# Six parts of each query and key row laid out in DRAM by the stores, and a group's rows loaded in two transfers

## The chip, the cores and the metric

The kernel runs on one core of a Trainium2 chip. The core has a matrix engine (TensorE, PE in the profile), a vector engine (VectorE, DVE), an activation engine (ScalarE, ACT), a general engine (GpSimd, POOL) and SyncE (SP), from whose queue nearly all DMA transfers of this kernel are issued, one after the other; the transfers themselves are carried by 16 DMA engines. The metric is the device time of one execution in microseconds, and the median of several executions is compared.

## The reference

Two independent layers are computed and their results set side by side along the last axis. A is attention in four segments with a compressive memory, for 32 heads of 18 dimensions over 2048 positions; B is a Fourier mixing layer over the same shape (2048 x 576).

```python
def _A_ref(x, wq, wk, wv, wo, beta):
    B, S, D = x.shape
    H = 32; Dh = D // H; N = 4; L = S // N
    # q, k, v: x @ w, as (B, H, N, L, Dh)
    ...
    for s in range(N):
        qs, ks, vs = q[:, :, s], k[:, :, s], v[:, :, s]
        logits = jnp.einsum("bhqd,bhkd->bhqk", qs, ks) * scale + mask
        p = _softmax(logits, axis=-1)
        a_dot = jnp.einsum("bhqk,bhkd->bhqd", p, vs)
        pq = phi(qs)
        num = jnp.einsum("bhld,bhde->bhle", pq, M)
        den = jnp.einsum("bhld,bhd->bhl", pq, z)[..., None] + 1e-6
        o = g * (num / den) + (1.0 - g) * a_dot
        outs.append(o)
        pk = phi(ks)
        M = M + jnp.einsum("bhld,bhle->bhde", pk, vs)
        z = z + jnp.einsum("bhld->bhd", pk)
    ...
    return o @ wo

def _B_ref(x, dft_seq_re, dft_seq_im, dft_hid_re, dft_hid_im):
    a = jnp.einsum("bsd,ed->bse", x, dft_hid_re)
    b = jnp.einsum("bsd,ed->bse", x, dft_hid_im)
    return jnp.einsum("ts,bse->bte", dft_seq_re, a) - jnp.einsum("ts,bse->bte", dft_seq_im, b)
```

All inputs and the output are float32, so the kernel splits operands into high and low parts and adds several products.

## The kernel before

**Projections** (lines 435 to 479). For each of the four segments s of 512 positions, nine tiles m of query and key rows are projected (`project_qk`, line 236: m from 0 to 3 queries, 4 to 7 keys, 8 the last 64 rows of both) and then the values of four blocks j of 128 positions (`project_v`, line 276), from the second segment on with the look-ups in the memory (`lookup`, line 331) between them. The result of a tile m stands in a PSUM bank (four banks with the tag "acc"), and ACT and POOL cut it into three bfloat16 parts that add up to it: `p[:, 0]` (line 247), `p[:, 1]` (256 or 258) and `p[:, 2]` (259). `p` has four buffers. The three parts go to DRAM in one store per tile, to `qd[s]` or `kd[s]`, of shape [576, 3, 512] (lines 261 to 264); the tile m = 8 has one store for each.

**Attention** (`attention`, line 805) works in 32 groups G of four heads, 8 groups for each segment, and 64 pairs of heads (two pairs to a group) plus four steps that drain the pipeline. Scores are one bfloat16 matmul over 108 rows for each piece of a head: the six products of parts that matter (query parts 0, 0, 1, 0, 2, 1 against key parts 0, 1, 0, 2, 0, 1; QPARTS and KPARTS, lines 32 and 33) are stacked below each other, 6 x 18 = 108 rows. `stack_load` (line 420) fetches this stack for a group: six transfers of 18 rows x 4 heads x 512 for the query stack `qs` and six for the key stack `ks`, each row 1 KB. There are four buffers of each; three more rows of `qs` take the maxima of the scores, which go through DRAM (`maxima_transpose`, line 719: a store `md<-mt` and later a load `qs<-md`), against rows of ones in `ks` that POOL sets (line 403).

A head with an even number is scored a second time with keys on the partitions (`t_fill`, line 727), for which it needs the maxima in `qs`; one with an odd number is scored again with queries on the partitions (`f_fill`), and its probabilities are transposed by a DMA transpose on SyncE (`f_turn`, line 706), which waits for both halves of `f_split_lo`, on POOL and on DVE. `pv` (line 765) multiplies the probabilities with the values `vst`, which the `values` part of `stack_load` fetches.

**Order.** The order on every engine is the order in which the program emits instructions. `later(n, fn)` (line 82) puts work n ticks off; `tick()` runs what is due. In the projections there is one tick for each tile m and each block j. In attention each step p has eight slots with a tick after each (lines 815 to 859), and after each slot a stretch of the Fourier layer (`dense`, line 573) is emitted until the shares of both agree; its inputs come through `c_load` (`craw`, four buffers, line 373) and are cut by `c_cut`. SyncE runs its queue strictly in order: a transfer that waits for an engine holds up all transfers emitted behind it.

`stack_load` is called for group 0 in the last segment after the seventh of the nine tiles (n = 6), with one query and one key part in each of the six following ticks (`each=1`), and in attention at the first slot of every even step p, for group p/2 + 1, with two of each in each of three ticks. The values of a group follow `lag` ticks after the call. `f_turn` is called in the last slot of a step.

Of the kernel before, what the change touches and what calls it, by code (L numbers as in the profile page):

```python
# [15 lines left out]
BF16 = mybir.dt.bfloat16  # L16
# [7 lines left out]
P = 128  # L24
# [4 lines left out]
HEAD0 = [0, 7, 14, 21, 24]  # L29
NPAIR = 108  # L30
BF16_ONES = float(np.array([0x3F803F80], np.uint32).view(np.float32)[0])
QPARTS = [0, 0, 1, 0, 2, 1]
KPARTS = [0, 1, 0, 2, 0, 1]


@with_exitstack
def infini_attention_and_fnet(ctx: ExitStack, tc: tile.TileContext, xT, wqk, w8, wv, wo, beta, xtT, cT, hT, out):
# [5 lines left out]
    dram = ctx.enter_context(tc.tile_pool(name="dram", bufs=1, space=DRAM))  # L43
    wide = ctx.enter_context(tc.tile_pool(name="wide", bufs=32))

    qd = [dram.tile([D, 3, L], BF16, name=f"qd{s}") for s in range(NSEG)]
    kd = [dram.tile([D, 3, L], BF16, name=f"kd{s}") for s in range(NSEG)]
    vd = [dram.tile([P, 4, 8, 220], BF16, name=f"vd{s}") for s in range(NSEG)]
    amd = [dram.tile([P, D], F32, name=f"amd{t}") for t in range(NT)]
    md = [dram.tile([24, P], BF16, name=f"md{g}") for g in range(32)]  # L50
# [171 lines left out]
    def open_qk(s):  # L222
# [4 lines left out]
        for a, b in zip(edges, edges[1:]):  # L227
# [5 lines left out]
            if s and a == 0:  # L233
                accumulate(3, (0, 1))

    def project_qk(s, m):
        if m in FIRST:
            o = FIRST.pop(m)
        else:
            o = ps.tile([P, L], F32, name="qk", tag="acc", bufs=4)  # L240
            chain(o, qk_terms(s, m))
        if m >= 4 and s < 3:
            KF[m] = sk.tile([P, L], F32, name="kf", bufs=5)
            act.activation(KF[m], o, AF.Copy)
        p = sb.tile([P, 3, L], BF16, name="p", bufs=4)
        r = sb.tile([P, L], F32, name="r", bufs=2)
        act.activation(p[:, 0], o, AF.Copy)
        dve.tensor_tensor(r, o, p[:, 0], OP.subtract)
        if s and (m < 4 or m == 8):
            n = P if m < 4 else 64  # L250
            c = m if m < 4 else 4
            phi(sb, "q", o[:n], n, pq_hi[:n, c], pq_lo[:n, c])

        def rest():
            if m in (5, 6, 7):
                pool.tensor_copy(p[:, 1], r)
            else:
                act.activation(p[:, 1], r, AF.Copy)
            pool.tensor_tensor(p[:, 2], r, p[:, 1], OP.subtract)
            if m < 8:  # L260
                later(1, dma, (qd if m < 4 else kd)[s][(m % 4) * P:(m % 4 + 1) * P], p)
            else:
                later(1, dma, qd[s][4 * P:], p[:64])
                later(1, dma, kd[s][4 * P:], p[64:])

        later(1, rest)

# [149 lines left out]

    NG = 32

    def stack_load(G, lag=39, each=2):  # L420
        if G >= NG:
            return
        s, g8 = divmod(G, 8)
        rows = slice(g8 * 72, g8 * 72 + 72)
        for buf, src, parts in ((qs_bufs[G % 4], qd[s], QPARTS), (ks_bufs[G % 4], kd[s], KPARTS)):
            for c, part in enumerate(parts):
                later(1 + c // each, dma, buf[18 * c:18 * c + 18],
                      src[rows, part, :].rearrange("(h d) t -> d h t", d=DH))

        def values():  # L430
            VS[G] = sa.tile([P, 4, 220], BF16, name="vst", bufs=2)
            dma(VS[G], vd[s][:, :, g8])
        later(lag, values)

    for s in range(NSEG):
        more = s < 3
        if s == 0:
            warm_up()
        open_qk(s)
        if s:  # L440
            memory()
        else:
            tick()
        for n, m in enumerate((0, 1, 2, 3, 8, 4, 5, 6, 7) if s else range(9)):
            project_qk(s, m)
            tick()
            if not more and n >= 5:
                h_split(0, n - 5)
            if s in (1, 2) and n >= 4:
                load_x(s + 1, n - 4)  # L450
            if not more and n == 0:
                for k in range(5):
                    h_load(0, k)
            if not more and n == 4:
                p1k.close()
                sr = ctx.enter_context(tc.tile_pool(name="sb2r", bufs=1, side="right", reuse_waits="tile"))
                attention_tiles()
            if not more and n in (5, 6):
                stacks(sr, n - 5)
            if not more and n == 5:  # L460
                c_load(0)
            if not more and n == 6:
                stack_load(0, 99, 1)
        for j in range(4):
            project_v(s, j, lookup(s, j) if s else iter(()))
            if more:
                k_natural(j)
            tick()
            for k in ((0, 1), (2, 3), (4,), ())[j] if s == 0 else ():
                load_x(1, k)  # L470
            if more and j in (1, 2):
                split_x(s + 1, j - 1)
            if not more and j < 3:
                h_split(0, 4) if j == 0 else c_cut(j - 1, dve)
            if not more:
                c_load(1 + j)
            if more and j:
                accumulate(j - 1)
# [326 lines left out]
    def attention():  # L805
        for p in range(NP + V_LAG):
            def even(lag, fn, *a):
                if 0 <= p - lag < NP:
                    fn(2 * (p - lag), *a)

            def odd(lag, fn, *a):
                if 0 <= p - lag < NP:
                    fn(2 * (p - lag) + 1, *a)

            if p == 2:
                stacks(sa, 2)
                stacks(sa, 3)
            if p == NP + 1:
                o_load(0)
                o_load(1)  # L820
            if p % 2 == 0:
                stack_load(p // 2 + 1)
            if p % 2 == 0 and 0 < p <= NP:
                maxima_transpose(p // 2 - 1)
            even(T_LAG + 1, t_lo, 0)
            even(0, s_fill, 0)
            odd(F_LAG + 1, f_exp, 2)
            odd(F_LAG + 1, f_split_hi)
            yield SLOTS[0]
            even(T_LAG, t_fill, 0)  # L830
            even(T_LAG, t_fill, 1)
            yield SLOTS[1]
            even(0, s_fill, 1)
            odd(F_LAG + 1, f_split_lo, pool, 512, 1280)
            yield SLOTS[2]
            even(V_LAG, pv)
            even(0, s_fill, 2)
            odd(F_LAG + 1, f_split_lo, dve, 0, 512)
            even(T_LAG, t_mask)
            yield SLOTS[3]  # L840
            odd(F_LAG, f_fill, 1)
            even(T_LAG, t_fill, 2)
            if p % 2 and p < NP:
                maxima(p // 2)
            yield SLOTS[4]
            odd(F_LAG, f_fill, 0)
            even(T_LAG, t_hi)
            yield SLOTS[5]
            odd(V_LAG, pv)
            odd(F_LAG, f_fill, 2)  # L850
            odd(F_LAG, f_exp, 1)
            even(T_LAG, t_lo, 1)
            even(T_LAG, t_lo, 2)
            yield SLOTS[6]
            odd(F_LAG, f_exp, 0)
            if p >= V_LAG:
                pv_out(p - V_LAG)
            odd(F_LAG + 1, f_turn)
            yield SLOTS[7]

    d = dense()
# [75 lines left out]
```

## Time and profile before

| | |
|---|---|
| median of three runs | 1028.67 us (1027.47 to 1031.02) |
| the profiled execution, its time | 1030.27 us |
| the profiled execution, span from first to last instruction | 1028.5 us |
| granted TensorE clock, mean over the span | 0.997 |
| TensorE busy | 1007.7 us (98%) |
| DVE, ACT, POOL busy | 705.9, 715.0, 624.2 us |
| stores of query and key parts (qd<-p, kd<-p) | 20 + 20 |
| loads of query and key stacks (qs<-qd, ks<-kd) | 192 + 192, of 72 KB |
| loads of maxima (qs<-md), DMA transposes (ptt<-hl) | 32, 64 |

In the rows of the timeline the first number is the start in us from the first instruction, the second the length, then engine, line, operation, output and inputs, the number of instructions merged into the row, and in brackets how long the engine had been idle and what released it. SPq is SyncE's queue; its rows are the times in which it issues a transfer, not those in which data move. In a table of windows the columns are the stretch, the busy time (with the number of instructions) of PE, PEld (weight loads), DVE, ACT and POOL, the granted clock of TensorE (PEclk), the mean busy share of the 16 DMA engines, and what they moved in GB/s. In a list of waits stand the total in us, the number of times and the longest.

### The profile page before, as it was taken

How to read it: one execution, taken by the hardware profiler on the slowest of the kernel's cores; microseconds unless marked ns; L12 is line 12 of the kernel's file. 1: busy time of each engine (PE TensorE's matmuls, PEld its weight loads, DVE VectorE, ACT ScalarE, POOL GpSimd, SP SyncE). 2: the span in 40 equal slices, each digit the busy share in tenths (PEclk: the TensorE clock that was granted, in tenths of full speed). 3: DMA queues.
4: the chain of work that ended last, by engine and by line, in shares of the span. 5: the costliest groups of instructions: out<-in, count | busy, mean ns of one | idle time of the engine just before them, and what ended most of it. 6: DMA issues, size and time to landing. Idle time of an engine off the chain costs nothing.

```text
span 1028.5 us, 25886 instructions
## 1 busy us (share of the span) xinstructions
PE 1007.7 (98%) x9464; PEld 942.5 (92%) x9464; DVE 705.9 (69%) x1903; ACT 715.0 (70%) x1654; POOL 624.2 (61%) x668
## 2 busy tenths in 40 slices
PE   9999999989999999999999999999999999999998
PEld 7989989889999999998998999999999889999998
DVE  6645557563677777778888777777777778885442
ACT  6657575653777787877878788877677777876333
POOL 2657575775666677676766867666667567666000
PEclk9999999998999999999999999999999999999999
DMA  7516243375568887898998987689998899977574
GB/s 250 186 65 204 88 159 147 128 242 151 154 157 190 199 207 197 210 218 193 221 215 194 217 188 182 164 202 226 224 217 195 202 242 234 235 176 182 156 209 137
DMA packets 287743, 194.46 MB, mean 189 GB/s; under 512 B 210496, under 2 KB 242816, under 8 KB 287616
## 3 DMA queue, kind: packets, MB, share of 16 engines
q1 hardware_dynamic: 287616, 192.81, 73.5%
q8 instruction: 74, 1.21, 0.5%
q14 instruction: 53, 0.43, 0.1%
HBM read 106.84 MB, written 43.97 MB: 147 GB/s over the span
## 4 chain that ended last, share of the span: by engine, by line
PE 83%; DMA 7%; ACT 2%; POOL 2%; DVE 2%; SPq 2%; issue 1%; POOLq 0%; ACTq 0%; DVEq 0%
PE d L493 31%; PE qk L78 6%; PE s L664 6%; PE d L78 6%; PE qk L230 5%; PE v L78 4%; PE pv L780 4%; PE d L539 3%; PE d L540 3%; PE d L541 3%; DMA qs<-md 2%; PE pv L781 2%; PE m L314 2%; DMA ptt<-hl 2%; DMA ks<-kd 2%; PE look L339 1%
## 5 line engine op out<-in xcount | busy, mean ns | idle before, releaser
L670 DVE CUSTOM_DVE_ANT_0 s<-s,causal 128x128 f32<-128x128 f32 (+3 forms) x512 | 251.7, 498 | 119.9 <-PE s L664 108.6
L393 POOL TENSOR_TENSOR clo<-craw,chi 128x512 fp32r<-128x512 f32 x158 | 209.6, 1327 | 161.4 <-ACT chi L388 128.1
L493 PE MATMUL d<-wide,chi 128*128 128x288 f32 x1408 | 266.7, 306 | 0.0
L493 PEld LDWEIGHTS d<-wide,chi 128*128 128x128 f32 x1408 | 212.3, 189 | 1.3 <-issue 0.2
L493 PE MATMUL d<-wide,clo 128*128 128x288 f32 x704 | 178.0, 319 | 0.0
L664 PE MATMUL s<-ks,qs 108*128 108x128 bf16 (+3 forms) x512 | 134.2, 304 | 6.7 <-DMA ks<-kd 4.3
L704 POOL TENSOR_TENSOR hl<-pf,hl 128x768 f16<-128x768 f32 x64 | 110.2, 1723 | 48.5 <-ACT hl L700 39.8
L693 ACT ACTIVATE pf<-s,nb 128x128 f32<-128x128 f32 (+3 forms) x256 | 128.3, 527 | 6.2
L493 PE MATMUL d<-ab,chi 128*128 128x288 f32 x640 | 126.1, 306 | 0.0
L748 ACT ACTIVATE phi<-t 128x384 f16<-128x384 f32 x128 | 62.3, 487 | 83.7 <-PE t L745 83.7
L493 PEld LDWEIGHTS d<-wide,clo 128*128 128x128 f32 x704 | 119.0, 189 | 1.0
L388 ACT ACTIVATE chi<-craw 128x512 fp32r<-128x512 f32 x160 | 100.6, 630 | 8.1 <-DMA craw<-cT 3.3
L763 DVE TENSOR_TENSOR plo<-pf,phi 128x384 f16<-128x384 f32 (+1 forms) x128 | 105.0, 821 | 0.0
L749 ACT ACTIVATE pf<-t 128x384 f32<-128x384 f32 (+1 forms) x192 | 100.1, 521 | 3.8 <-PE t L738 3.7
L493 PEld LDWEIGHTS d<-ab,chi 128*128 128x128 f32 x640 | 98.5, 189 | 0.4
L700 ACT ACTIVATE hl<-pf 128x768 f16<-128x768 f32 (+1 forms) x128 | 87.4, 729 | 2.0
L539 PE MATMUL d<-wide,chi 128*128 128x288 f32 x256 | 85.6, 334 | 0.0
L493 PE MATMUL d<-ab,clo 128*128 128x288 f32 x320 | 84.9, 314 | 0.0
L540 PE MATMUL d<-wide,chi 128*128 128x288 f32 x256 | 76.5, 299 | 0.0
L541 PE MATMUL d<-wide,clo 128*128 128x288 f32 x256 | 76.4, 299 | 0.0
L763 POOL TENSOR_TENSOR plo<-pf,phi 128x384 f16<-128x384 f32 x64 | 61.3, 957 | 11.5 <-ACT pf L749 10.7
L704 DVE TENSOR_TENSOR hl<-pf,hl 128x512 f16<-128x512 f32 x64 | 62.9, 982 | 0.7 <-ACT hl L700 0.5
(196 smaller groups left out, 2522.8 us busy)
## 6 DMA issues: line engine op xcount, KB each, us to landing
craw<-cT SPq DMA_DIRECT2D x128, 256.0 KB
qs<-qd SPq DMA_DIRECT2D x192, 72.0 KB
ks<-kd SPq DMA_DIRECT2D x192, 72.0 KB
craw<-xtT SPq DMA_DIRECT2D x32, 320.0 KB
out<-y SPq DMA_DIRECT2D x31, 288.0 KB
vd<-vs SPq DMA_DIRECT2D x16, 440.0 KB
vst<-vd SPq DMA_DIRECT2D x32, 220.0 KB
qd<-p SPq DMA_DIRECT2D x16, 384.0 KB
```

The costliest lines, as they stand in the source:

```text
L78: pe.matmul(o, a, b, start=n == 0, stop=n == len(terms) - 1)
L388: act.activation(hi, raw[:, :4], AF.Copy)
L393: engine.tensor_tensor(lo, raw[:, :4], hi.bitcast(F32), OP.subtract)
L493: pe.matmul(o[h], a, b[:, h * 288:h * 288 + 288], start=start, stop=stop)
L539: pe.matmul(o, xh[:, k], wl[k][:, cs], start=k == 0, stop=False)
L540: pe.matmul(o, xh[:, k], wh[k][:, cs], start=False, stop=False)
L541: pe.matmul(o, xl[:, k], wh[k][:, cs], start=False, stop=False)
L664: pe.matmul(o[:, c:c + w], q[:, i * P:w], k[:, :w], start=True, stop=True)
L670: dve.tensor_tensor_reduce(o[:, c:c + w], o[:, c:c + w], CAUSAL[0][:, L - w:], scale=scale, scalar=-LOWEST, op0=OP.add, op1=OP.min, accum_ ...
L693: act.activation(f[:, FIRST_COL[i]:FIRST_COL[i] + w], o[:, c:c + w], AF.Exp, bias=nb[:, i:i + 1], scale=-1.0)
L704: engine.tensor_tensor(hl[:, 1, a:b], f[:, a:b], hl[:, 0, a:b], OP.subtract)
L763: (pool if kind == 2 else dve).tensor_tensor(lo[:, a:b], f[:, a:b], hi[:, a:b], OP.subtract)
```

## The change

The arrays in DRAM get six parts for each row in place of three, in the order in which the stacks need them; the stores write a part as often as it occurs, with a source that repeats. The query stack's order is now 0, 1, 2, 0, 1, 0 and the key stack's 0, 0, 0, 1, 1, 2, which makes the same six products. In QPARTS and KPARTS each tuple is (first place, first part, number of parts, copies). In the first segment a query tile is stored once, with three parts, and each key part once; four transfers from DRAM to DRAM, emitted in the second segment after its first four tiles, fill the other places.

A group's stack is then 108 rows of DRAM at one step, and `stack_load` is one transfer for queries and one a tick later for keys. Its calls move: group 0 to the fifth tile of the last segment, group 1 to the first slot of step 0, the others from the first slot of an even step to the seventh slot of the odd step before it. `f_turn` moves from the end of the last slot to the start of the seventh, ahead of that call. `lag` becomes 41, two ticks more, as the call comes two ticks earlier. The stack buffers 2 and 3 are made at steps 1 and 2.

```diff
-QPARTS = [0, 0, 1, 0, 2, 1]
-KPARTS = [0, 1, 0, 2, 0, 1]
+
+QPARTS = ((0, 0, 3, 1), (3, 0, 2, 1), (5, 0, 1, 1))
+KPARTS = ((0, 0, 1, 3), (3, 1, 1, 2), (5, 2, 1, 1))
...
-    qd = [dram.tile([D, 3, L], BF16, name=f"qd{s}") for s in range(NSEG)]
-    kd = [dram.tile([D, 3, L], BF16, name=f"kd{s}") for s in range(NSEG)]
+    qd = [dram.tile([D, 6, L], BF16, name=f"qd{s}") for s in range(NSEG)]
+    kd = [dram.tile([D, 6, L], BF16, name=f"kd{s}") for s in range(NSEG)]
...
+    def store_parts(key, s, row, p):
+        to = (qd, kd)[key][s][row:row + p.shape[0]]
+        for at, part, n, copies in (QPARTS, KPARTS)[key]:
+            if s == 0 and not key and at:
+                continue
+            c = copies if s else 1
+            dma(to[:, at:at + n * c], p[:, part:part + n].to_broadcast([p.shape[0], n * c, L]) if c > 1 else p[:, part:part + n])
+
+    def copy_parts(i):
+        to, at, n, first, copies = ((qd[0], 3, 2, 0, 1), (qd[0], 5, 1, 0, 1), (kd[0], 1, 1, 0, 2), (kd[0], 4, 1, 3, 1))[i]
+        a = to[:, first:first + n]
+        dma(to[:, at:at + n * copies], a.to_broadcast([D, copies, L]) if copies > 1 else a)
...
             if m < 8:
-                later(1, dma, (qd if m < 4 else kd)[s][(m % 4) * P:(m % 4 + 1) * P], p)
+                later(1, store_parts, m >= 4, s, (m % 4) * P, p)
             else:
-                later(1, dma, qd[s][4 * P:], p[:64])
-                later(1, dma, kd[s][4 * P:], p[64:])
+                later(1, store_parts, 0, s, 4 * P, p[:64])
+                later(1, store_parts, 1, s, 4 * P, p[64:])
...
-    def stack_load(G, lag=39, each=2):
+    def stack_load(G, lag=41):
...
-        for buf, src, parts in ((qs_bufs[G % 4], qd[s], QPARTS), (ks_bufs[G % 4], kd[s], KPARTS)):
-            for c, part in enumerate(parts):
-                later(1 + c // each, dma, buf[18 * c:18 * c + 18],
-                      src[rows, part, :].rearrange("(h d) t -> d h t", d=DH))
+        for i, (buf, src) in enumerate(((qs_bufs[G % 4], qd[s]), (ks_bufs[G % 4], kd[s]))):
+            later(1 + i, dma, buf[:NPAIR], src[rows].rearrange("(h d) c t -> (d c) h t", d=DH))
...
+            if s == 1 and n < 4:
+                copy_parts(n)
...
-            if not more and n in (5, 6):
-                stacks(sr, n - 5)
+            if not more and n == 4:
+                stacks(sr, 0)
+                stack_load(0, 99)
             if not more and n == 5:
                 c_load(0)
             if not more and n == 6:
-                stack_load(0, 99, 1)
+                stacks(sr, 1)
...
-            if p == 2:
-                stacks(sa, 2)
-                stacks(sa, 3)
+            if p == 0:
+                stack_load(1, 39)
+            if p in (1, 2):
+                stacks(sa, p + 1)
...
-            if p % 2 == 0:
-                stack_load(p // 2 + 1)
...
             yield SLOTS[5]
+            odd(F_LAG + 1, f_turn)
+            if p % 2:
+                stack_load((p + 3) // 2)
             odd(V_LAG, pv)
...
-            odd(F_LAG + 1, f_turn)
             yield SLOTS[7]
```

## The prediction

> **What bounds the kernel now.** I read the head of the page first, then who TensorE waited for, then the one long wait and the periodic ones on the timeline.
>
> ```profile
> span 1028.5 us, 25886 instructions
> ...
> PE 1007.7 (98%) x9464; PEld 942.5 (92%) x9464; DVE 705.9 (69%) x1903; ACT 715.0 (70%) x1654; POOL 624.2 (61%) x668
> ...
> qs<-qd SPq DMA_DIRECT2D x192, 72.0 KB
> ks<-kd SPq DMA_DIRECT2D x192, 72.0 KB
> ```
>
> TensorE is busy for 1007.7 of 1028.5 us, and the change leaves its matmuls alone. So a gain must come out of 20.8 us of idle time, or out of matmuls that run at a lower clock. The last two rows are the transfers that the change merges: 192 + 192 of 72 KB, 12 for each of 32 groups. Who ended TensorE's idle time, in us, times, longest:
>
> ```profile
> PE s L664 <- DMA ks<-kd: 4.3, 1, 4.3
> PE t L738 <- DMA qs<-md: 3.9, 6, 0.9
> PE pv L780 <- DMA ptt<-hl: 2.4, 2, 1.7
> PE s L664 <- DVE negm L670: 2.3, 3, 0.9
> ...
> PE trm L721 <- POOL mb L717: 1.4, 1, 1.4
> ```
>
> Three of the first four are transfers: one wait of 4.3 us for key rows, six for the maxima that go through DRAM into the query stack (qs<-md), two for the transposed probabilities (ptt<-hl). Together 10.6 us. What DVE and POOL cost, 3.7 us, the change does not touch.
>
> The long wait lies between the projections and attention. TensorE's timeline, then SyncE's:
>
> ```profile
> 227.45 0.28 PE L339 MATMUL look<-mdh,pq_lo 128*128 128x152 f32 x1
> 232.06 0.58 PE L664 MATMUL s<-ks,qs 108*128 108x512 bf16 x1 [4.34 <-DMA ks<-kd]
> ```
>
> ```profile
> 225.42 0.34 SPq L88 DMA_DIRECT2D amd<-am  x1
> 226.69 0.34 SPq L88 DMA_DIRECT2D vd<-vs  x1
> 227.09 0.42 SPq L378 DMA_DIRECT2D craw<-xtT  x1
> 227.56 0.64 SPq L88 DMA_DIRECT2D qs<-qd  x1
> 228.24 0.35 SPq L88 DMA_DIRECT2D ks<-kd  x1
> ```
>
> Group 0's rows are loaded in six ticks, one query and one key part in each, and the last part stands in SyncE's order behind stores of the value projection that wait for POOL. It is issued at 228.24 and the first score starts at 232.06. The clock pays for that idle time too; the columns end with PEclk, DMA share and GB/s:
>
> ```profile
> 230.00:232.00 2.00, 0.00 (x0) 0.00 (x0) 1.02 (x1) 0.00 (x0) 2.00 (x2) 0.79 0.36 124
> 232.00:234.00 2.00, 1.94 (x8) 1.88 (x9) 0.78 (x2) 0.00 (x0) 1.82 (x3) 0.50 0.82 294
> ...
> 236.00:238.00 2.00, 2.00 (x11) 1.85 (x10) 0.52 (x2) 0.41 (x1) 0.00 (x0) 0.50 0.69 164
> 238.00:240.00 2.00, 2.00 (x17) 1.93 (x17) 1.38 (x6) 0.90 (x3) 0.00 (x0) 1.00 0.62 155
> ```
>
> From 232 to 238 the granted clock is 0.50, and 11 matmuls start in 2 us where 17 do afterwards.
>
> Then the steady state of attention. SyncE's queue round one of the six waits for the maxima, and TensorE's row:
>
> ```profile
> 728.50 0.72 SPq L88 DMA_DIRECT2D qs<-qd  x2
> 729.26 0.69 SPq L88 DMA_DIRECT2D ks<-kd  x2
> 730.06 0.30 SPq L88 DMA_DIRECT2D md<-mt  x1
> 730.41 1.04 SPq L88 DMA_DIRECT2D qs<-qd  x2
> 731.90 0.79 SPq L88 DMA_DIRECT2D ks<-kd  x2
> 733.30 0.62 SPq L378 DMA_DIRECT2D craw<-cT  x1
> 734.02 0.38 SPq L88 DMA_DIRECT2D od<-og  x1
> 734.45 0.77 SPq L88 DMA_DIRECT2D qs<-qd  x2
> 735.26 0.77 SPq L88 DMA_DIRECT2D ks<-kd  x2
> 736.07 0.75 SPq L88 DMA_DIRECT2D qs<-md  x1
> ...
> 737.39 0.59 SPq L432 DMA_DIRECT2D vst<-vd  x1
> 738.08 3.94 SPq L709 DMA_TRANSPOSE ptt<-hl  x1
> ```
>
> ```profile
> 739.66 0.40 PE L738 MATMUL t<-qs,ks 111*128 111x128 bf16 x4 [0.51 <-DMA qs<-md]
> ```
>
> SyncE issues almost without a gap. Between the store of the maxima (730.06) and the load that brings them back (736.07) stand eight stack loads, and TensorE waits for that load. The transpose at 738.08 starts 0.10 us after the load before it ends: there SyncE, and not its data, is late.
>
> **The change part by part.** *Group 0's load moves up.* It becomes two transfers, called after the fifth projection of the last segment, not six ticks from the seventh. They land long before TensorE ends the projections at 227.73, so the 4.34 us go. What is late next is the emptying of PSUM: the last look-up matmul ends at 227.73, and its banks are still being read for some time. In the old run that reading lies under the wait. The last reader on DVE:
>
> ```profile
> 229.06 0.19 DVE L352 TENSOR_TENSOR w<-look,g 128x32 f32<-128x32 f32 x1
> ```
>
> It ends at 229.25, so what stays lies between 0 (the scores get other banks) and 1.5 us; I take 0.8: gain 3.5 us (2.8 to 4.3). With no long idle time the clock should hold: (238 − 232.06) × 0.5 = 3.0 us (0 if a shorter gap triggers it as well).
>
> *Ten of twelve issues go in each group.* The six rows of loads above are 0.72 + 0.69 + 1.04 + 0.79 + 0.77 + 0.77 = 4.78 us of SyncE. No load of 432 pieces of 1 KB is in the trace; the lower bound of its issue is a single small load, about 0.36 (0.72 for two), the upper is six of them, 2.4. The nearest row is vst<-vd, which also brings many short pieces in one transfer: 0.59. I take 0.6, so two cost 1.2, and SyncE gets 3.6 us of each group back. The pair is also moved ahead of the maxima's store, so eight loads, 1.04 + 0.79 + 0.77 + 0.77 = 3.37 us, leave the stretch between store and reload. The reload can then go out 2 to 3 us earlier, and the six waits are at most 0.9 us each: all 3.9 us of them can go, and most of the 2.4 us for transposes. Ends: 0 (if the transfers themselves and not their issue set the landing; their bytes stay the same) and 6.3 us. I take 5.0, since a queue with no gap between issues speaks for the upper end.
>
> One rule of the Trainium skill speaks against this: "DMA: Bandwidth & Descriptors", section "Issuing engines are not separate DMA queues", says of the sequencer's issue time that it is usually small beside the transfer. By it this term would be 0 and not 5.0. The rows above show 4.78 us of issue for one group's 12 loads, which is not small here. The same page, section "Why a DMA increments its semaphore by 16 and not by 1", gives the number of engines of a transfer as the largest divisor up to 16 of its outer size: 9 for 18 rows, 12 for 108. That would spread the loads better; no row here shows it, and no term uses it.
>
> *The transposes are called a slot earlier and group loads stand right behind them.* SyncE waits at a transpose for POOL and DVE; queued behind it now are the spectral loads (craw), vst, od and y transfers of the last two slots, and the stack pair itself, which is due more than two pair-steps later. craw has four buffers and the stacks four, so I cost this at nothing; without that cover it costs what the transposes take on SyncE, 4 us at a time.
>
> *The projections' stores become three, and copies are added.* From the second segment on each store of p becomes three, and its bytes double. In the first segment query parts get one, key parts three, and four DRAM-to-DRAM copies of 576 rows (6 KB of each row pair in all) fill in the rest during the second segment. The cost is in how soon a p buffer (four) comes free. The rows for the second segment, ACT, SyncE, DVE, TensorE, and a stretch of the stores alone:
>
> ```profile
> 90.41 0.60 ACT L247 ACTIVATE p<-qk 128x512 bf16<-128x512 f32 x1 [1.66 <-DMA kd<-p]
> ```
>
> ```profile
> 87.57 0.58 SPq L88 DMA_DIRECT2D kd<-p  x1
> ```
>
> ```profile
> 91.10 0.69 DVE L248 TENSOR_TENSOR r<-qk,p 128x512 f32<-128x512 f32 x1 [2.04 <-ACT p L247]
> ```
>
> ```profile
> 92.47 0.23 PE L339 MATMUL look<-mdl,pq_hi 128*128 128x152 f32 x1
> ```
>
> ```profile
> 72.00:76.00 4.00, 4.00 (x20) 3.30 (x19) 1.73 (x3) 3.11 (x7) 3.45 (x4) 1.00 0.25 98
> ```
>
> ACT already waits here for the store issued at 87.57. DVE empties the bank at 91.79, and TensorE's look-up at 92.47 is the first that could want it: 0.7 us of cover. That projection's two stores become six, four more at about 0.36 = 1.4 us; its bytes rise by 384 KB, at 98 / 0.25 = 392 GB/s another 1.0 us. Of up to 2.4 us the cover takes 0.7; issue and transfer overlap, so I take 0.8 us for each of three segments, 2.5 in all (0 to 3 × 1.7 + 1 for the copies = 6). The copies themselves ride on engines that are a quarter busy.
>
> *Sum:* −3.5 − 3.0 − 5.0 + 2.5 = −9.0 us. The profiled execution took 1030.27 us, 1.6 above the median of the runs; it would become 1021.3, and the median 1028.67 − 9.0 = 1019.7, say 1020.
>
> **The rivals.**
> (a) *Transfers, not issue.* The landing of maxima and transposes is set by bytes ahead of them, which don't change, so the attention term is 0. For it: 3.55 us pass from the load at 736.07 to TensorE's start, longer than its issue. Against: the gapless queue. Time 1028.67 − 6.5 + 2.5 = 1024.7. The skill's sentence on issue time, above, belongs here.
> (b) *The first score waits for the next thing,* for instance the PSUM banks or a value store pushed back by the larger key stores, and the transition gains nothing; attention gives 3. For it: SyncE there waits for POOL anyway (1.27 us between the issues at 225.42 and 226.69). Time 1028.67 − 3 + 2.5 = 1028.
> (c) *Slower: the p buffers.* If a tripled store holds ACT's p for as long as the old wait for key rows, TensorE stops over 4 us in each of three segments and the clock halves after each: 3 × (4.3 + 3.0) = 22 us, less the 11.5 of gains, 1039. It decides from a delay of about 4 us behind a cover of 0.7; the rows give 2.4.
> (d) *More than forecast.* All 10.6 us of transfer waits and the clock go, the stores cost nothing: 1028.67 − 13.6 = 1015.
>
> **How the numbers follow.** Forecast 0.55, (a) 0.17, (b) 0.10, (c) 0.10, (d) 0.08. The forecast's own range is 1015 to 1024. From 1013, (d) less the spread of runs (1027.47 to 1031.02), to 1029, above (a) and (b), lies about 0.8; (c) is left out. A measurement here tells 0.3%, 3.1 us, from no change. Faster by more: the forecast, (d) and most of (a), 0.75; within: the rest of (a) and most of (b), 0.15; slower: 0.10.
>
> **What would show it.** In the changed profile: TensorE's wait for ks<-kd at the first score is gone or under 1.5 us and the granted clock stays 1.00 there; 32 + 32 stack loads, each about 0.6 us on SyncE; qs<-md drops out of TensorE's waits; ACT p L247 waits longer for kd<-p, and TensorE's idle time in the projections rises by 2 to 3 us. Wrong would be: waits for maxima that stay with a shorter queue (a), a new releaser of the first score (b), or half clock inside the projections (c).

## The result, and the profile after

The changed kernel is slower by 0.8%: a median of 1039.12 us in five runs (1036.26 to 1040.50) against 1031.02 us (1027.47 to 1032.21) for the kernel before on the same chip, a ratio of 1.0083 with a 95% interval of 1.0056 to 1.0109. The profiled execution spans 1037.4 us in place of 1028.5, +8.9 us.

The head of its page:

```profile
span 1037.4 us, 25645 instructions
...
PE 1013.6 (98%) x9464; PEld 948.4 (91%) x9464; DVE 706.4 (68%) x1903; ACT 714.8 (69%) x1654; POOL 623.9 (60%) x668
...
qs<-qd SPq DMA_DIRECT2D x32, 432.0 KB
ks<-kd SPq DMA_DIRECT2D x32, 432.0 KB
```

The change did what it says: 32 + 32 loads in place of 384. TensorE does the same 9464 matmuls but is busy 5.9 us longer, so part of the loss is matmuls at a lower clock: the mean granted clock is 0.990, before 0.997. The page doesn't say where. Reading the stages off TensorE's timeline does (us; the three columns after the name are the starts of the last three segments' projections):

| | seg. 2 | seg. 3 | seg. 4 | last look-up ends | first score starts | output projection starts | span |
|---|---|---|---|---|---|---|---|
| before | 57.5 | 116.0 | 174.4 | 227.7 | 232.1 | 958.2 | 1028.5 |
| after | 57.6 | 122.3 | 184.3 | 245.0 | 244.9 | 967.1 | 1037.4 |

The projections lose 17.3 us, all of it from the second segment on, where the stores are doubled; the first segment is unchanged. In the trace TensorE stands still for 9.6 us more there than before, and three stretches of half clock (92.3 to 99.1, 160.6 to 164.0, 235.7 to 242.5, where before has none) take some 8.5 us; the two overlap a little. The transition wins 4.5 us back (4.3 of waiting became −0.2, the two overlap), attention 3.8 us (726.1 became 722.3), the tail nothing (70.3 both times): 17.3 − 4.5 − 3.8 = 9.0.

Who ended TensorE's idle time in the changed kernel, then the rows of its timeline:

```profile
PE look L353 <- DVE r L262: 4.1, 3, 1.6
PE v L79 <- DVE vr L308: 4.1, 2, 3.7
PE s L679 <- ACT pf L708: 4.0, 3, 2.7
PE v L79 <- DVE r L262: 2.1, 2, 1.9
```

```profile
91.51 0.34 PE L353 MATMUL look<-mdl,pq_hi 128*128 128x152 f32 x1 [1.61 <-DVE r L262]
94.89 0.85 PE L79 MATMUL v<-wide,xh 128*128 128x288 f32 x2 [1.89 <-DVE r L262]
...
158.99 0.34 PE L353 MATMUL look<-mdl,pq_hi 128*128 128x152 f32 x1 [1.62 <-DVE r L262]
...
236.78 0.85 PE L79 MATMUL v<-wide,xh 128*128 128x288 f32 x2 [3.71 <-DVE vr L308]
...
244.75 0.27 PE L353 MATMUL look<-mdh,pq_lo 128*128 128x152 f32 x1
244.86 0.39 PE L679 MATMUL s<-ks,qs 108*128 108x512 bf16 x1
```

The old waits for key rows and maxima have left the head of the list, and the first score follows the last look-up without a gap. In their place stand waits for DVE (`r`, `vr`). DVE is not slow: it waits for ACT, and ACT for a buffer whose store has not landed. ACT's timeline shows the releasers:

```profile
90.06 0.60 ACT L261 ACTIVATE p<-qk 128x512 bf16<-128x512 f32 x1 [3.10 <-DMA qd<-p]
...
219.33 0.60 ACT L261 ACTIVATE p<-qk 128x512 bf16<-128x512 f32 x1 [4.35 <-DMA kd<-p]
...
235.75 0.42 ACT L305 ACTIVATE vs<-v 128x288 bf16<-128x288 f32 x1 [6.28 <-DMA vd<-vs]
```

The last row matters: `vs` is a buffer of the value projection, and the change doesn't touch its store. The chain of waits, followed back within the ends of the second and the fourth segment (start, length, what), says how long these transfers took:

```profile
85.00 8.35 DMA qd<-p
...
220.75 7.96 DMA kd<-p
...
230.36 5.28 DMA vd<-vs
```

Eight microseconds from issue to landing for a store of parts: the largest of them, three parts of 128 rows, is 384 KB, 1.0 us at the prediction's 392 GB/s. That they stand behind other bytes is what the windows suggest. In those of the changed kernel, and of the one before for the same stretch, the last two columns are the share of the DMA engines and GB/s, the one ahead of them TensorE's clock:

```profile
84.00:88.00 4.00, 4.00 (x19) 3.30 (x19) 1.35 (x3) 2.13 (x5) 3.23 (x3) 1.00 1.03 366
88.00:92.00 4.00, 2.39 (x19) 2.16 (x18) 0.69 (x1) 1.08 (x2) 0.80 (x2) 1.00 1.05 379
92.00:96.00 4.00, 2.11 (x11) 1.90 (x11) 0.69 (x1) 1.08 (x2) 2.30 (x4) 0.54 0.84 220
96.00:100.00 4.00, 4.00 (x23) 4.00 (x23) 2.02 (x5) 2.72 (x8) 2.53 (x3) 0.61 0.97 332
```

```profile
84.00:88.00 4.00, 4.00 (x20) 3.34 (x19) 1.81 (x4) 3.17 (x7) 3.38 (x3) 1.00 0.65 166
88.00:92.00 4.00, 4.00 (x34) 4.00 (x33) 1.68 (x4) 2.34 (x6) 3.80 (x6) 1.00 0.85 200
92.00:96.00 4.00, 4.00 (x35) 4.00 (x34) 2.32 (x9) 2.75 (x8) 2.16 (x3) 1.00 1.02 386
```

Before, the DMA engines were filling up by 92 us (0.65, 0.85, 1.02) and TensorE didn't notice. After, they are full from 84 on, TensorE stands still for 3.5 us between 88 and 96, and from 92 to 100 its clock is 0.54 and 0.61, a further 3.4 us lost (8 us at a mean of 0.58). Less their overlap, that makes the second segment's +6.2 us.

In attention SyncE's timeline round the store of the maxima (md<-mt) and the load that brings them back (qs<-md), and the list of SyncE's waits, show what became of the saved issues:

```profile
563.15 0.39 SPq L89 DMA_DIRECT2D ks<-kd  x1
563.64 0.39 SPq L89 DMA_DIRECT2D md<-mt  x1
564.13 0.35 SPq L89 DMA_DIRECT2D od<-og  x1
564.58 0.38 SPq L392 DMA_DIRECT2D craw<-cT  x1
570.60 0.74 SPq L89 DMA_DIRECT2D qs<-md  x1
```

```profile
SPq L89 <- DMA md<-mt: 117.4, 32, 5.6
```

The reload needs the store to have landed. With only two transfers left to issue in between, SyncE stands for 5.6 us here; it waits in all 32 groups, 117.4 us in all, 3.7 us in each: all that was saved. The inputs of the Fourier layer queue behind it: ACT's waits for `craw` (from cT) rise from 3.3 to 14.7 us.

### The profile page after: what moved, and what is told of

Its sections match the earlier page's. It is cut to its first block, busy times and chain, and to the rows that moved or that the text cites. A ratio compares the mean times of both kernels' runs of the same rounds, so it can differ in the third digit from the quotient of the medians.

```text
span 1037.4 us, 25645 instructions
## 1 busy us (share of the span) xinstructions
PE 1013.6 (98%) x9464; PEld 948.4 (91%) x9464; DVE 706.4 (68%) x1903; ACT 714.8 (69%) x1654; POOL 623.9 (60%) x668
## 3 DMA queue, kind: packets, MB, share of 16 engines
q8 instruction: 74, 1.21, 0.5%
## 4 chain that ended last, share of the span: by engine, by line
PE 77%; DMA 9%; ACT 6%; POOL 3%; DVE 2%; issue 2%; SPq 1%; POOLq 0%; ACTq 0%; DVEq 0%
PE d L508 32%; PE s L679 6%; PE d L79 6%; PE v L79 4%; PE pv L795 4%; PE qk L231 3%; PE d L554 3%; PE d L555 3%; PE d L556 3%; PE pv L796 2%; DMA craw<-cT 2%; PE m L328 2%; PE qk L79 2%; DMA craw<-xtT 1%; PE look L353 1%
## 5 line engine op out<-in xcount | busy, mean ns | idle before, releaser
L402 ACT ACTIVATE chi<-craw 128x512 fp32r<-128x512 f32 x160 | 100.6, 630 | 26.4 <-DMA craw<-cT 14.7
L778 DVE TENSOR_TENSOR plo<-pf,phi 128x384 f16<-128x384 f32 (+1 forms) x128 | 107.2, 838 | 1.4 <-ACT phi L773 1.4
```

The source lines that it names most:

```text
L402: act.activation(hi, raw[:, :4], AF.Copy)
L778: (pool if kind == 2 else dve).tensor_tensor(lo[:, a:b], f[:, a:b], hi[:, a:b], OP.subtract)
```

## The experiments

All ratios are against runs of the kernel before on the same chip, with 95% intervals. The letters in the expectations name theories, each with what it expects. The main ones: S, a p buffer is held until its longer store lands; I, the number of issues on SyncE does it; B, the doubled bytes fill the transfer queue; W, SyncE's saved time is lost in the wait for md<-mt. The edits are against the changed kernel unless another is named.

**Copies later.** The four copies from DRAM to DRAM leave the query and key tiles of the second segment for its value blocks.

```diff
-            if s == 1 and n < 4:
-                copy_parts(n)
...
             project_v(...)
+            if s == 1:
+                copy_parts(j)
```

> The changed kernel, with the four DRAM-to-DRAM copies emitted after the four value blocks of the second segment and not after its first four tiles. Theory S (the p buffers are held by stores that queue behind other bytes): the second segment, which grew by 6.2 us against 3.6 us for the third, falls to about the third's growth, so about 2.6 us less than the changed kernel, near 1036. Rival I (three issues in place of one on SyncE hold the buffers): the copies take only four issues, the time stays within 1 us of the changed kernel.

Measured: 1041.40 us, ratio 1.0104 (1.0070 to 1.0139); the time rises, which neither theory expected. A stall of 1.58 us for a late `r` stays at 93.8, ahead of the first copy (issued at 99.53), and a longer one comes at 115.27, the end of the second segment; TensorE's timeline:

```profile
115.27 1.26 PE L328 MATMUL m<-vnh,knl 128*128 128x152 f32 x5 [4.09 <-POOL knl L205]
```

POOL in turn waits 24.7 us (13.2 in the changed kernel) for the store of the memory, amd<-am. So the stall at 94 doesn't need the copies, and the copies collide with whatever is stored beside them.

**More p buffers.** Every fifth and sixth tile takes one of two further buffers.

```diff
-        p = sb.tile([P, 3, L], BF16, name="p", bufs=4)
+        turn[0] += 1
+        if s < 3 and turn[0] % 6 > 3:
+            p = sk.tile([P, 3, L], BF16, name="p", bufs=2)
+        else:
+            p = sb.tile([P, 3, L], BF16, name="p", bufs=4)
```

> The changed kernel with six p buffers in the first three segments (the fourth segment keeps four). Theory S: the wait of ACT p for a store's landing goes in the second and third segments, whose growth of 6.2 + 3.6 us falls to under 2, so about 8 us less than the changed kernel, near 1031. Rival I: SyncE itself is late, so later transfers (values, look-ups) are late as well, and less than 3 us come back.

Measured: 1039.37 us, 1.0086 (1.0056 to 1.0116), no gain. In the second and third segments, which have the six buffers, ACT's waits for one are down to a single 0.6 us; these waits have grown in their place, with TensorE's longest stall behind them:

```profile
POOL am L374 <- DMA amd<-am: 25.4, 3, 10.9
...
ACT vs L311 <- DMA vd<-vs: 22.1, 4, 9.0
```

```profile
114.22 1.26 PE L334 MATMUL m<-vnh,knl 128*128 128x152 f32 x5 [6.25 <-POOL knl L205]
```

S falls here: the p buffers are the first to notice, not the cause. With more of them SyncE runs further ahead, and the next stores with few buffers, of the memory (`am`, one buffer) and of values, wait instead. The time fits theory I as well, which the next runs test.

**Bytes alone, issues alone, and the group 0 load alone**, each on the kernel before:

```diff
# before_bytes: as many stores, every byte twice, from the second segment on
+        if s:
+            dma(to.rearrange("p (r c) t -> p r c t", r=2), p[:, None].to_broadcast([p.shape[0], 2, 3, L]))
# before_issues: the same bytes, three stores of one part each
+        if s:
+            for c in range(3):
+                dma(to[:, c], p[:, c])
# before_early0: group 0's twelve loads called two tiles earlier
-            if not more and n == 6:
-                stack_load(0, 99, 1)
+            if not more and n == 4:
+                stack_load(0, 99, 6)
```

> The kernel before, with each store of a tile in the second to fourth segments writing its three parts twice (6 KB a row in place of 3, still one issue, 3 KB pieces); all else as before. Theory B (the doubled bytes fill the transfer queue, and whatever store comes next is late): the projections' last look-up ends 6 to 12 us later than before, the total 5 to 10 us longer. Rival I (the number of issues): no change, within 2 us.

> The kernel before, with each store of a tile in the second to fourth segments cut into three, one for each part (1 KB pieces), the same bytes as before. Theory B: within 2 us of the kernel before. Rival I: the projections end 6 us or more later.

> The kernel before, with group 0's twelve loads emitted in the two ticks after the fifth tile of the last segment. Both theories: the 4.3 us wait of the first score goes and the clock stays up, 5 to 7 us faster, unless the loads, which stand in front of the key stores there, push the end of the projections out (theory G: last look-up 2 us or more later, gain under 3 us).

Measured: bytes 1036.61 us, 1.0054 (1.0038 to 1.0070), and the projections 8.2 us longer (last look-up at 235.9); issues 1032.40 us, 1.0012 (0.9993 to 1.0030), projections +0.8; early load 1027.44 us, 0.9967 (0.9947 to 0.9986), the first score at 228.1 in place of 232.1. So B holds, and I falls as a cause by itself: three issues for the same bytes cost next to nothing, bytes cost 8.2 us. And the transition's gain needs only the earlier call, not the new layout. It came to 3.2 us in the median, under the 5 to 7 expected: half a microsecond went to the projections, and attention took 727.4 us in place of 726.1 in the profiled executions, although its start was at full clock.

**All the stores of the change, without its copies and its loads** (on the kernel before, with its twelve loads reading the new places):

```diff
+    def store_parts(key, s, row, p):
...
-                later(1, dma, (qd if m < 4 else kd)[s][(m % 4) * P:(m % 4 + 1) * P], p)
+                later(1, store_parts, m >= 4, s, (m % 4) * P, p)
```

> The kernel before with the changed kernel's stores alone (three for each tile, each part as often as it occurs, key pieces of 1 KB), no copies, the twelve loads of a group as before, reading each part where it stands. Doubled bytes in one store of 3 KB pieces put the last look-up at 235.9 us (227.7 before), a third of the bytes in each of three stores at 228.5. Theory B alone: 235 to 238, since the pieces cost little by themselves. If pieces and bytes work together: 240 to 243, what the changed kernel's 245.0 leaves after the copies' 2 to 3 us.

Measured: 1040.77 us, 1.0100 (1.0068 to 1.0133). The projections are 12.2 us longer, 4.0 more than by the bytes alone; their end at 239.9 lies between the two forecasts. TensorE's stall for a late `r` in the second segment, here and then with the bytes alone, and the windows right behind the one and the other:

```profile
94.45 0.34 PE L348 MATMUL look<-mdl,pq_hi 128*128 128x152 f32 x1 [1.58 <-DVE r L257]
```

```profile
93.65 0.34 PE L345 MATMUL look<-mdl,pq_hi 128*128 128x152 f32 x1 [1.21 <-DVE r L254]
```

```profile
96.00:100.00 4.00, 4.00 (x23) 4.00 (x21) 2.93 (x9) 2.64 (x5) 2.69 (x3) 0.58 1.01 309
```

```profile
96.00:100.00 4.00, 4.00 (x35) 4.00 (x34) 2.95 (x6) 2.48 (x7) 3.03 (x3) 1.00 1.04 404
```

The engines are full in both. The stall is 0.4 us longer, and behind it the clock falls to 0.58 and 23 matmuls start where 35 do. With that the second segment takes 1.8 us more than with the bytes alone; the third, where the same happens (a stall of 1.65 us at 156.4), 2.6 us more, and the fourth 0.9 us less. Half clock is not the whole of it: this is the slowest of five executions (1045.61 us, mean clock 0.990), and two with a mean clock of 0.997 and 0.998 still took 1040.8 and 1040.4 us. Whether the pieces of 1 KB or the three issues cost the rest, no run tells.

**Copies first.** The four copies are emitted at the start of the second segment, ahead of `memory()`.

```diff
+        if s == 1:
+            for i in range(4):
+                copy_parts(i)
...
-            if s == 1 and n < 4:
-                copy_parts(n)
```

> The changed kernel with its four copies all emitted before the second segment's tiles, when the transfer engines are idle, and not among its stores. Theory B: the second segment grows by about what the third does (3.6 us in place of 6.2), the time is 2 to 3 us under the changed kernel's. If the copies were not what made the second segment longer than the third: within 1 us.

Measured: 1033.14 us, 1.0028 (1.0005 to 1.0050); the last look-up ends at 241.07, 3.9 us earlier than in the changed kernel. The copies among the stores therefore cost some 2.4 to 3.9 us (the same projections end at 245.0 in the changed kernel and at 243.5 and 244.0 in the next two), most of it in the second segment, which takes 62.1 us in place of 64.6. The sum for the projections: bytes 8.2, three stores with key rows in pieces of 1 KB 4.0, copies in that place 3.9, and 1.2 left for the rest (17.3 − 8.2 − 4.0 − 3.9), group 0's earlier load among it (0.5 in the run with that alone). Each term is from one execution and good to about 1.5 us, by that spread. The median gained 6 us and not 3.9; attention took 718.9 us here and 722.3 in the changed kernel with the same code, which lies within the spread told below.

**The order in attention.** The pair of loads goes back to the first slot, so that it is issued behind the store of the maxima (the transposes keep their new place); then the transposes go back too.

```diff
# md_cover
+            if p and p % 2 == 0:
+                stack_load(p // 2 + 1, 39)
...
-            if p % 2:
-                stack_load((p + 3) // 2)
# cover_turn: the same, and
-            odd(F_LAG + 1, f_turn)
...
             (end of the last slot)
+            odd(F_LAG + 1, f_turn)
```

> The changed kernel with the two stack loads called behind the maxima's store (first slot of the even step, as before the change), so that they stand in the stretch in which SyncE waits for that store to land. Theory W (what SyncE saved in issues it lost in a wait of 117 us in 32 pieces for md<-mt): this wait falls to under 40 us in total, the waits of ACT chi for craw<-cT (14.7 us) and of TensorE behind them fall, 2 to 4 us less than the changed kernel. Rival F (the maxima's reload is late whatever stands in front): TensorE's waits for qs<-md come back and the time stays within 1 us or rises.

> The run with the stack loads behind the maxima's store, with the transposes back in the last slot, as before the change. Theory W (the wait for the maxima's store was what took attention's gain): attention from the first score stays within 2 us of 716. Rival T (the earlier transpose is itself worth something or costs something): it moves by more than 2 us, longer if early transposes help, shorter if they hold up the spectral loads.

Measured: 1032.58 us, 1.0015 (1.0002 to 1.0028), and 1031.36 us, 1.0005 (0.9990 to 1.0020). Attention takes 715.8 and 715.3 us. The first one's timeline of SyncE and its wait:

```profile
560.71 0.35 SPq L89 DMA_DIRECT2D md<-mt  x1
561.12 0.35 SPq L89 DMA_DIRECT2D qs<-qd  x1
561.52 0.45 SPq L89 DMA_DIRECT2D ks<-kd  x1
562.07 0.44 SPq L89 DMA_DIRECT2D od<-og  x1
562.61 0.60 SPq L392 DMA_DIRECT2D craw<-cT  x1
565.15 0.74 SPq L89 DMA_DIRECT2D qs<-md  x1
```

```profile
SPq L89 <- DMA md<-mt: 7.4, 10, 1.9
```

With the two loads behind the store the waits go from 117.4 to 7.4 us. Covering them is the smaller part: the two issues take 0.80 us in the rows above, some 26 us in 32 groups, of the 110 that went. The store also lands sooner. Over all 32 groups the reload goes out a median of 5.65 us after its store in the changed kernel, where the pair was issued just ahead of the store, and 2.63 us after it here. The pair brings 864 KB, 2.3 us at 392 GB/s (an estimate); that the store waited for these bytes fits the rows, but no run moves the bytes alone.

W holds for SyncE, and the median falls by 6.5 and 7.8 us, more than the 2 to 4 expected; 1.0 to 1.5 us of it are shorter projections in the profiled executions. TensorE gains some 5 us in attention (the mean of 720.8 us over four kernels with the changed kernel's attention, which took 716.8 to 725.2, less 715.6). The place of the transposes makes no difference that these runs can tell.

**No larger layout.** Three parts in DRAM as before, and a stack in four transfers each: one of 54 rows, three of 18 rows at every third partition.

```diff
-            later(1 + i, dma, buf[:NPAIR], src[rows].rearrange("(h d) c t -> (d c) h t", d=DH))
+            later(1 + i, dma, buf[at:at + 54], src[rows].rearrange("(h d) c t -> (d c) h t", d=DH))
+            for c, part in enumerate(parts):
+                later(1 + i, dma, buf[54 - at + c:108 - at:3], src[rows, part].rearrange("(h d) t -> d h t", d=DH))
```

> One store of three parts for each tile as before, no copies, a group's stack in eight transfers (54 + 3 x 18 rows for queries and for keys, another order of the same six products), group 0 early, the stack loads behind the maxima's store, the transposes a slot earlier. Theories B and W: projections as before (last look-up near 228), first score at once, attention near the 716 us of the run with the loads behind the store (726 before), total 1014 to 1019. If attention needs the two-transfer form: over 1021.

Measured: 1036.53 us, 1.0053 (1.0034 to 1.0072). The projections cost nothing now (last look-up at 228.6, as expected), but attention takes 738.8 us, and the forecast of 1014 to 1019 is missed. Against the kernel before attention lost 12.7 us, and 9.0 of it show in TensorE's waits for the maxima, which rise from 3.9 us to these 12.9:

```profile
PE t L739 <- DMA qs<-md: 12.9, 11, 3.1
```

The reload goes out a median of 7.2 us after its store here, nearly all of it spent on issues. The loads of `qs` by SyncE's issue time (ns; least, median, most), here and in the changed kernel:

```profile
L88 SPq DMA_DIRECT2D qs<-qd x128: 294/746/1393, 205.0 to 889.3; - x128
```

```profile
L89 SPq DMA_DIRECT2D qs<-qd x32: 392/542/1469, 217.4 to 884.9; - x32
```

Four issues merged into a row take 2.76 and 2.74 us in the steady state, so eight cost 5.5 us, more than the 4.78 of the twelve they replace. An issue has no fixed price. Its shape changes it: 54 adjacent rows take 0.30 to 0.49 us here, 18 rows at every third partition 0.75, and 18 adjacent rows 0.34 in the kernel before. So does the moment: with the bytes alone, stores of one shape take a median of 0.52 us for queries and 1.27 for keys, which come later.

**Copies only.** The projections store each part once, and all four segments' other places are filled by copies: of the first two segments among the value blocks of the next, of the last two in attention.

```diff
+        dma((qd, kd)[key][s][row:row + p.shape[0], 3 * key:3 * key + 3], p)
...
+            if s in (1, 2):
+                copy_parts(s - 1, j)
...
+            if p >= 6 and p % 2 == 0 and p < 22:
+                copy_parts(2 + (p - 6) // 8, (p - 6) // 2 % 4)
```

> The changed kernel with one store of three parts for each tile, as before the change, in all segments (query places 0 1 2 1 0 0, key places 0 1 0 0 1 2), and the three missing places filled by four DRAM-to-DRAM copies for each segment: those of the first two after the value blocks of the next segment, those of the last two in steps 6 to 20 of attention. Theory S or I alike: the projections fall back from 245.0 to near 228 us, first score at once; attention as in the changed kernel, plus what 7 MB of copies cost there (0 to 4 us). Time 1039 - 17 + 2 = about 1024. Rival A (attention's wins were only lower clock losses): the same projections but over 1030.

Measured: 1033.03 us, 1.0021 (1.0003 to 1.0039). The projections are back at 228.3: with single stores, copies among the value blocks cost next to nothing. But attention, with eight copies in its first twenty steps, takes 736.8 us in the profiled execution, which is 4 us above the median, and the forecast of 1024 is missed; the time is where rival A put it. But not only the clock lengthens it: SyncE waits 125.2 us for md<-mt, as in the changed kernel, and TensorE 7.7 us for the reload, up to 3.2 at a time. How much of it the copies cost, this run can't tell.

**The version that beats both.** The same copies, each segment's all at the start of the next one, the last segment's spread over attention, and the load pair behind the maxima's store.

```diff
+        if s:
+            for i in range(4):
+                copy_parts(s - 1, i)
         (memory() of the segment)
...
+            if p and p % 2 == 0:
+                stack_load(p // 2 + 1, 39)
...
+            if p in (9, 17, 25, 33):
+                copy_parts(3, (p - 9) // 8)
```

> One store of three parts for each tile, as before; the missing places filled by DRAM-to-DRAM copies where the transfer engines are nearly idle: those of a segment before the next segment's tiles (all four at once), those of the last segment one by one in steps 9, 17, 25 and 33 of attention; two transfers for a group, issued behind the maxima's store; group 0 early. Theories B and W: last look-up near 228, first score at once, attention near 716 us (716 in the run with the loads behind the store, 726 before) plus up to 4 for the copies: 1017 to 1021, faster than both. If the copies collide with the tiles' stores after all, the last look-up comes at 232 or later and the time is over 1024.

Measured: 1019.15 us, ratio 0.9877 (0.9863 to 0.9892). The span is 1017.7 us, with TensorE busy for 1004.1. The transition on TensorE's timeline, and the windows in which the copies run:

```profile
229.65 0.28 PE L346 MATMUL look<-mdh,pq_lo 128*128 128x152 f32 x1
229.76 0.39 PE L672 MATMUL s<-ks,qs 108*128 108x512 bf16 x1
```

```profile
60.00:64.00 4.00, 4.00 (x24) 3.49 (x24) 1.22 (x2) 0.00 (x0) 1.69 (x3) 1.00 0.79 241
64.00:68.00 4.00, 4.00 (x21) 3.35 (x21) 0.41 (x1) 1.40 (x4) 1.08 (x3) 1.00 1.00 295
68.00:72.00 4.00, 4.00 (x19) 3.30 (x18) 2.00 (x4) 2.84 (x5) 3.73 (x9) 1.00 1.05 343
```

The engines are as full as in the changed kernel at 88, and TensorE stays at 4.00 of 4 us: at a segment's start it waits for nothing that these copies hold up. The third and fourth segments start as before (115.7 and 174.2 us against 116.0 and 174.4); the last look-up ends at 229.9, 2.2 us later than before, with 1.7 us of new short stalls (0.84 and 0.82) and no half clock. Attention takes 717.5 us.

## Why the prediction was wrong

**The step that failed** is "The projections' stores become three, and copies are added", priced at 2.5 us (0 to 6); it came to 17.3. It failed in three ways. It took the load of the DMA engines from one window, 72 to 76, at a share of 0.25; the trace of before has 0.65, 0.85 and 1.02 for the later windows of the same segment, shown above. It delayed one tile's store by its own extra bytes, where the bytes of all tiles add up: 1152 rows of 3 KB are 3.5 MB more in a segment, an estimated 9 us of all 16 engines at 392 GB/s; the runs put the doubled bytes at 8.2 us over the three segments. And it followed only the p buffers, not the stores of values and memory that stand in the same queue behind them. "The copies themselves ride on engines that are a quarter busy" is the same error: they cost some 2.4 to 3.9 us more in that place than at the segment's start.

**Rival (c)** named the right side and place, and the median nearly (1039), but by another sum: it asked for stalls over 4 us. Only one stall was near that (3.71 us, behind a value store); two of 1.6 us were followed by half clock as well. The projections lost 17.3 and not 22 us, and the p buffers are not the cause.

**The transition** went as forecast: the wait of 4.34 us is gone (I had kept 0.8 us of it, and nothing stayed), and the clock is full there. But a half-clock stretch stands just ahead of it, behind the value projection's stall of 3.71 us, as the windows of the changed kernel show:

```profile
240.00:244.00 4.00, 4.00 (x25) 4.00 (x24) 0.68 (x2) 0.93 (x2) 1.34 (x2) 0.69 0.71 243
244.00:248.00 4.00, 4.00 (x33) 3.90 (x33) 2.95 (x8) 2.64 (x7) 1.21 (x1) 1.00 0.13 52
```

**"SyncE gets 3.6 us of each group back"** was true of the issues and wrong of the time: 3.7 us in each group went into waiting for md<-mt. Taking the eight loads out from between store and reload was to send the reload out 2 to 3 us earlier. It went out later: a median of 4.96 us after its store before, 5.65 after, and 2.63 with the pair behind the store (6.0, 7.0 and 4.4 us in the rounds shown). The step that failed here is the place of the pair: two loads of 432 KB just ahead of the store whose landing the reload needs.

**Attention, −5.0:** measured −3.8, and up to 3.0 of it is the half clock at before's start ((238 − 232.06) × 0.5), which the changed kernel's attention doesn't have. TensorE's waits for qs<-md and ptt<-hl fell as forecast, from 3.9 and 2.4 us to 1.0 and 0.2, though the reload follows its store later; why, the runs don't show. In their place came 4.0 us of waits for ACT (`pf`), the longest, 2.70 us at 823.15, behind ACT's wait of 4.04 us for craw, with half clock from 822.8 to 826.2. One execution can't size this term: four kernels with the same attention code took 716.8 to 725.2 us (mean 720.8), five with twelve loads in before's order 725.2 to 729.3 (727.3). By the means the gain is 6.5 us, at most 3.0 of it the clock at the start, so 3.5 to 6.5 for this term: that it lies round the 5.0 forecast is partly luck, as SyncE's saved time went into the wait for md<-mt. (The 3.55 us that rival (a) names is 3.59 by the rows it rests on.)

**The rule of the Trainium skill** on issue time, weighed in the prediction ("DMA: Bandwidth & Descriptors", section "Issuing engines are not separate DMA queues"), did not decide: 4.78 us of issue in a group is not small here, and the eight dearer ones went with a longer attention, but the changed kernel saved most of its issue time and lost it in a wait. What the same section says first, that transfers run on the same 16 DMA engines and interleave there, whichever engine started them, would have been the one to weigh: the runs agree, with a value store of 5.28 us behind the doubled key stores.

## What to carry to other kernels

Before adding bytes to a stream of stores, read the share of the DMA engines over the whole stretch in which they run, its last part above all, and list every later transfer of the same queue whose buffer something waits for: more buffers for the first to notice only pass the stall on. Put extra traffic where the engines are idle and nothing due follows; there the copies of three segments cost 2.2 us here, group 0's earlier load included, where the changed kernel's projections had lost 17.3. Try a small store whose landing a load needs ahead of large transfers in the queue, not behind them: here the reload went out 3 us sooner; what is issued between the two costs nothing as long as the landing takes longer.

## What the runs showed of the hardware

Stalls of TensorE of 1.58 to 1.62 us in the projections were followed by stretches at half clock (0.54 to 0.61 in the windows shown); the one of 1.21 us with the bytes alone was not. Length alone doesn't decide: stalls of 1.65 us (copies first, at 156.3), 1.81 us (the transposes put back too, at 159.4) and 2.50 us (copies later, at 181.4) were not followed by one either. The Trainium skill, "TensorE: Matmul & The Clock Gate", section "Part 1: The HAM clock gate (the "warmup" mystery)", puts half clock behind an idle window of about 3.4 us; the stalls here are half as long, though other short gaps lie near them. What the condition is stays open, as does why an issue for 18 rows at every third partition costs about 0.75 us.
